# A fused windowed attention and feed-forward kernel: turning the probabilities by squares and through DRAM, with keys in classes of four

## The chip, the cores and the metric

The kernel runs on one core of a Trainium2 chip. A core has five engines that run side by side, each with its own instruction stream: TensorE (PE in the profile; PEld is its weight load) multiplies matrices out of SBUF into PSUM, VectorE (DVE), ScalarE (ACT) and GpSimd (POOL) work on tiles element by element, and SyncE (SP) issues the transfers between DRAM and SBUF. They wait for each other through semaphores. The metric is the device time of one execution in microseconds.

## The reference

What is computed, cut to what matters:

```
scores = q @ k^T / sqrt(64)                      # 8 batches x 8 heads, 576 tokens, head size 64
rel = pos_query - pos_key
heads 0-3: keep 0 <= rel < 32                    # a window
heads 4-7: keep 0 <= rel < 128 and rel % 4 == 0  # a window with dilation 4
attn = softmax(where(keep, scores, -1e9)) @ v
x = attn with the heads of a token side by side  # 4608 x 512
xn = x / sqrt(mean(x^2) + 1e-6) * rms_g
out = (silu(xn @ w_gate) * (xn @ w_val)) @ w_out # 512 -> 1536 -> 512
```

## The kernel before, in words

The 4608 tokens are cut into 16 units of 288 (half a batch). Attention and feed-forward are fused: while TensorE runs the feed-forward of one unit, the attention of the next is threaded between its matrix products.

The feed-forward of a unit runs over 12 blocks j of the hidden size. Each block has three parts, and each part is a **tick**: `gate` (12 large matmuls into the PSUM tile g), `val` (12 into v) and `proj` (12 into the four accumulators acc, for the block before). Large matmuls go in threes, since every fp32 operand is split into a high and a low part of a shorter type (L679 high by high, L682 the two mixed ones). So a unit has 36 ticks. Behind a gate ScalarE takes a tanh (L719) and VectorE makes of it a silu (L724); behind a val VectorE multiplies the two (L737, "the product"), ScalarE takes the high part (L748) and GpSimd the low part (L749). Two PSUM banks carry g and v in turns (`bank`): the gate of the next block is written where the val of this block lay, so it begins only when L737 has read it. The tile th has one buffer.

The attention of a unit is 14 **bursts** of two heads: for c = 0, 1 (window) three blocks of 96 queries each, with 128 keys (96 in the first block of an even unit); for c = 2, 3 (dilation) four residue classes of 72 queries, with 72 keys in even units and 104 in odd ones. Where a burst does its steps is written out by hand in ticks. `plan` puts the scores of burst k (s, L524) behind the large matmuls of tick −11 + 2k of its unit, the transposes (t, L497) 6 ticks later and the output (o, L512) 10 ticks later. So every second tick is heavy, with up to three such pieces on TensorE behind its 12 matmuls, and every other one light. What the other engines do is put off with `later(dt, rank, fn)`: `flush`, at the head of each tick, issues what is due in the order of rank. For a burst with its scores at tick n that is: n+1 the mask added to the low half of the scores (L381) and maximum (L386) on VectorE; n+2 two exponentials on ScalarE (L401); n+4 sum and reciprocal on VectorE (L410, L411) and scaling of the two heads on GpSimd (L417); n+6 two transposes on TensorE, through the matrix `ident`, into a PSUM tile (the free bank of g and v, or a tile t); a tick later `untranspose` copies it to SBUF as the high part (L477, ScalarE), and VectorE subtracts to make the low part (L479); n+10 the output, from high and low parts of probabilities (pt, two buffers) and of values (vhl, made by L320 on ScalarE and L324 on GpSimd); n+11 `take` adds the parts (L439, L441).

Queries and keys are loaded per head by SP (L293), and split by `split` into high and low: L349 and L354 for the keys (ScalarE, GpSimd), L358 and L363 for the queries. Values are loaded per burst (L301) into three buffers vt.

Units 0 to 2 run another way at the start (units with number below NEX = 3 keep exact probabilities, and their transposes). The 13 units from 3 on are the steady part. In them every engine's order is the order in which the program issues its instructions (a manual schedule).

## Time and profile before

| | us |
|---|---|
| median of three runs | 1104.16 (1103.92 to 1104.49) |
| the profiled execution's own time | 1103.95 |
| its span in the trace | 1102.2 |
| granted TensorE clock, mean | 1.0 of full speed |
| TensorE busy | 1095.2 |
| VectorE, ScalarE, GpSimd busy | 782.7, 614.8, 670.1 |
| bytes over the span | 73 GB/s |

The span runs from the first to the last record of the trace; the execution's own time is a little longer. A row of the grouped view names line, engine, operation, the tile written and the tiles read, shapes, count, then the sum of busy us and the mean ns of one, then the engine's idle time ahead of it. A row of the timeline gives start and duration in us; matmuls overlap in their pipeline, so for TensorE the distance from start to start tells what one costs.

### The profile page before, as it was taken

What the parts mean: (1) busy time and instruction counts of PE and PEld (TensorE: products, weight loads), DVE (VectorE), ACT (ScalarE), POOL (GpSimd) and SP (SyncE); (2) the same over time, 40 slices, a digit from 0 to 9 for tenths busy, and PEclk for the clock granted to TensorE, in tenths of its full rate; (3) what the DMA queues carried; (4) which work ended last, traced back from release to release, by engine and by line L of the source; (5) the groups of instructions that cost most, each with busy time, mean ns of one, the idle gap of its engine ahead of it and who ended that gap; (6) DMA issues with size and microseconds to landing.
All of it is one profiled execution on the core that took longest, in us unless ns stands there. A gap on an engine that the chain in (4) does not pass through costs nothing.

```text
span 1102.2 us, 25627 instructions
## 1 busy us (share of the span) xinstructions
PE 1095.2 (99%) x8416; PEld 1071.6 (97%) x8416; DVE 782.7 (71%) x3094; ACT 614.8 (56%) x2202; POOL 670.1 (61%) x1152
## 2 busy tenths in 40 slices
PE   8999999999999999999999999999999999999998
PEld 7787999999999999999999999999999999999998
DVE  7988667868687676867768677686867768687412
ACT  6895676556465564646556464664646556464211
POOL 6333589657585675757657575775758657584211
PEclk9999999999999999999999999999999999999999
DMA  9774213212131131312212131131212212120000
GB/s 255 205 263 163 79 51 87 74 35 82 43 94 52 41 97 30 95 42 73 66 36 85 43 94 43 50 96 37 79 43 83 64 32 83 53 74 13 18 6 22
DMA packets 61543, 82.18 MB, mean 75 GB/s; under 512 B 7298, under 2 KB 41090, under 8 KB 61410
## 3 DMA queue, kind: packets, MB, share of 16 engines
q1 hardware_dynamic: 61410, 80.54, 24.3%
q8 instruction: 67, 1.10, 0.4%
q14 instruction: 66, 0.54, 0.2%
HBM read 71.08 MB, written 9.44 MB: 73 GB/s over the span
## 4 chain that ended last, share of the span: by engine, by line
PE 95%; POOL 2%; DVE 1%; ACT 1%; issue 1%; POOLq 0%; ACTq 0%; DVEq 0%
PE acc L682 17%; PE g L682 17%; PE v L682 17%; PE acc L679 9%; PE g L679 9%; PE v L679 9%; PE o L512 3%; PE s L524 3%; PE acc L676 2%; PE v L676 2%; PE g L676 2%; PE t L497 2%; PE s L521 1%; PE g L497 1%; PE busy L802 1%; PE o L509 1%
## 5 line engine op out<-in xcount | busy, mean ns | idle before, releaser
L749 POOL TENSOR_TENSOR hlo<-th,hhi 128x288 fp32r<-128x288 f32 x179 | 145.2, 811 | 161.3 <-ACT hhi L748 147.8
L401 ACT ACTIVATE t<-t,sum 96x128 f32<-96x128 f32 (+3 forms) x448 | 165.9, 374 | 107.8 <-DVE sum L386 105.1
L682 PE MATMUL acc<-hhi,lo 128*128 128x288 f32 x720 | 212.7, 295 | 0.0
L417 POOL TENSOR_SCALAR t<-t,sum 96x128 f32<-96x128 f32 (+3 forms) x416 | 147.6, 366 | 88.4 <-DVE sum L411 74.6
L719 ACT ACTIVATE th<-g 128x288 f32<-128x288 f32 x180 | 73.8, 410 | 195.2 <-PE g L682 100.5
L682 PE MATMUL g<-xhi,lo 128*128 128x288 f32 x612 | 180.3, 295 | 0.0
L682 PE MATMUL v<-xhi,lo 128*128 128x288 f32 x612 | 180.2, 294 | 0.0
L439 DVE TENSOR_REDUCE xraw<-o 64x72 f32<-64x144 f32 (+1 forms) x364 | 117.1, 322 | 84.0 <-PE o L512 79.5
L724 DVE SCALAR_TENSOR_TENSOR th<-th,g 128x288 f32<-128x288 f32 x180 | 80.8, 449 | 102.0 <-ACT th L719 78.4
L682 PEld LDWEIGHTS acc<-hhi,lo 128*128 128x128 f32 x720 | 135.4, 188 | 0.0
L324 POOL TENSOR_TENSOR vhl<-vt,vhl 128x128 fp32r<-128x128 f32 x182 | 84.4, 464 | 70.4 <-ACT vhl L320 66.8
L748 ACT CAST hhi<-th 128x288 fp32r<-128x288 f32 x180 | 77.7, 432 | 75.5 <-DVE th L737 74.6
L682 PEld LDWEIGHTS g<-xhi,lo 128*128 128x128 f32 x612 | 115.2, 188 | 0.0
L682 PEld LDWEIGHTS v<-xhi,lo 128*128 128x128 f32 x612 | 115.1, 188 | 0.0
L737 DVE TENSOR_TENSOR th<-th,v 128x288 f32<-128x288 f32 x180 | 79.8, 444 | 43.6 <-PE v L682 43.5
L441 DVE TENSOR_TENSOR xraw<-o,xraw 64x72 f32<-64x72 f32 (+1 forms) x364 | 101.1, 278 | 12.5
L679 PE MATMUL acc<-hhi,hi_o 128*128 128x288 f32 x360 | 109.0, 303 | 0.0
L679 PE MATMUL g<-xhi,hi_g 128*128 128x288 f32 x357 | 107.0, 300 | 0.0
L682 PE MATMUL acc<-hlo,hi_o 128*128 128x288 f32 x360 | 106.4, 296 | 0.0
L363 POOL TENSOR_TENSOR qs<-qk,qs 64x288 fp32r<-64x288 f32 x104 | 84.3, 811 | 24.1 <-ACT qs L358 16.9
L354 POOL TENSOR_TENSOR ks<-qk,ks 128x288 fp32r<-128x288 f32 (+2 forms) x104 | 96.8, 936 | 3.1
L682 PE MATMUL g<-xlo,hi_g 128*128 128x288 f32 x322 | 95.1, 295 | 0.0
(193 smaller groups left out, 3458.6 us busy)
## 6 DMA issues: line engine op xcount, KB each, us to landing
qk<-in_qk_dram SPq DMA_DIRECT2D x60, 288.0 KB, 2.9
vt<-in_v_dram SPq DMA_DIRECT2D x196, 64.0 KB, 1.9
qk<-in_qk_dram SPq DMA_DIRECT2D x30, 352.0 KB, 2.9
out_dram<-ot SPq DMA_DIRECT2D x64, 144.0 KB, 1.9
qk<-in_qk_dram SPq DMA_DIRECT2D x30, 304.0 KB, 2.9
raw<-in_w_gate_dram SPq DMA_DIRECT2D x12, 512.0 KB, 4.6
...
```

The costliest lines, as they stand in the source:

```text
L324: G.tensor_tensor(out=vp[:, :, 1], in0=vs.pop(b), in1=vp[:, :, 0], op=ALU.subtract)
L354: ek.tensor_tensor(out=ks[:, 1, :nkt], in0=kr, in1=ks[:, 0, :nkt], op=ALU.subtract)
L363: eq.tensor_tensor(out=qs[D:], in0=qr[D:], in1=qs[D:], op=ALU.subtract)
L401: A.activation(out=t[:nq, a, :n], in_=t[:nq, a, :n], func=AF.Exp, scale=-1.0, bias=sm[:nq, a, 0:1], accum_out=None if by_rows(u, c, i) els ...
L417: (V if u == 0 and (c, i) > (NC - 1, 1) else G).tensor_scalar(out=t[:nq, a, :n], in0=t[:nq, a, :n], scalar1=sm[:nq, a, 3:4], scalar2=1.0, ...
L439: V.tensor_reduce(out=ours, in_=o[:D, cols:cols + 2 * nq].rearrange("d (t q) -> d q t", t=2), axis=mybir.AxisListType.X, op=ALU.add)
L441: V.tensor_tensor(out=ours, in0=o[D:, cols:cols + nq], in1=ours, op=ALU.add)
L679: PE.matmul(out, wh[:, cc, :], xh, start=start, stop=False)
L682: PE.matmul(out, w[:, cc, :], v, start=False, stop=stop and k == 1)
L724: V.scalar_tensor_tensor(out=t, in0=t, scalar=1.0, in1=g, op0=ALU.add, op1=ALU.mult)
L737: V.tensor_tensor(out=t, in0=t, in1=v_ps[:, :U], op=ALU.mult)
L749: (V if (u, j) == (NU - 1, NJ - 1) else G).tensor_tensor(out=lo, in0=t, in1=hi, op=ALU.subtract)
```

## The change

In units 3 to 15 the transposes on TensorE go. The scaled probabilities (a tile t of 96 queries by two heads by 128 keys) are turned in four steps instead. VectorE transposes t in place in squares of 32 x 32 (L514). SP writes it to a scratch tile in DRAM (L519). SP reads it back (L525) with the squares put in their places, in pieces of 32 floats: 128 partitions by 6 pieces. ScalarE makes the high part (L529), now from SBUF, and VectorE the low part (L533), now with both inputs in SBUF. The ticks are in `TURN`: squares and write at n+4, read-back at n+6, high part at n+8, low part at n+9, the output at n+10 as before. The scaling moves from n+4 to n+3.

In a square, 32 keys lie on 32 lanes, and the pieces that are read back hold, on each lane, the queries in a row. For this the 128 key places are seen as four classes of 32: the split of the keys (L351, L357) stores key 4i + c at place i of class c, the scores' matmul (L581) reads its keys by class, in runs of 18 to 32, and the mask is put into the same order once, ahead of unit 3. The tile t must hold no old numbers where a block has fewer than 96 queries or 128 keys: GpSimd zeroes it (L418) a tick ahead of the scores. vt goes from three buffers to two, and the loads of values and of queries and keys are issued a tick later.

The lines move: L737 is L799, L749 is L811, L719 L781, L724 L786, L679 and L682 are L741 and L744, L512 is L567, L524 L581, L439 and L441 L469 and L471, L381 L392, L386 L400, L401 L430, L410 and L411 L439 and L440, L417 L447, L293 L295, L301 L303.

```diff
-BEHIND = 6, 10
+OUTPUT = 10
+TURN = (4, 4), (4, 9.5), (6, 9.5), (8, 3), (9, -1.5)
...
+    dr = ctx.enter_context(tc.tile_pool(name="dr", bufs=2, space=bass.MemoryType.DRAM))
...
-            vt = sb.tile([P, 2, D], F32, tag="vt", name=f"vt_{u}_{c}_{i}", bufs=3)
+            vt = sb.tile([P, 2, D], F32, tag="vt", name=f"vt_{u}_{c}_{i}", bufs=2)
...
-            load_v(further(b, 3))
+            later(1, 9.9, lambda: load_v(further(b, 2)))
...
-            A.copy(out=ks[:, 0, :nkt], in_=kr)
+            A.copy(out=ks[:, 0, :nkt].rearrange("p (c k) -> p c k", c=4), in_=kr.rearrange("p (k c) -> p c k", c=4))
...
-            ek.tensor_tensor(out=ks[:, 1, :nkt], in0=kr, in1=ks[:, 0, :nkt], op=ALU.subtract)
+            hi, lo = (ks[:, t, :nkt].rearrange("p (c k) -> p c k", c=4) for t in range(2))
+            ek.tensor_tensor(out=lo, in0=kr.rearrange("p (k c) -> p c k", c=4), in1=hi, op=ALU.subtract)
...
-                load(*after(u, h, 2))
+                later(1, 9.9, lambda: load(*after(u, h, 2)))
...
+    def begin(b):
+        _, nq, _ = geometry(*b[:2])
+        n = geometry(*b[:2])[0][b[2]][3]
+        pool, bufs = (late[0], 1) if late and everything.index(b) % 4 == 3 else (sb, 3)
+        blank[b] = t = pool.tile([QB, 2, P], F32, tag="t", name=f"t_{b[0]}_{b[1]}_{b[2]}", bufs=bufs)
+        if nq < QB or n < P:
+            G.memset(t, 0.0)
...
-        def low_part():
-            V.tensor_tensor(out=pt[:n, 1, :, :nq], in0=t_in, in1=pt[:n, 0, :, :nq], op=ALU.subtract)
...
+    def turn(b):
+        blocks, nq, _ = geometry(*b[:2])
+        n = blocks[b[2]][3]
+        got = []
+
+        def squares():
+            t = st[b][0]
+            V.transpose(out=t, in_=t)
+
+        def put():
+            t, _ = st.pop(b)
+            d = dr.tile([2, QB, P], F32, tag="turn", name=f"turn_{b[0]}_{b[1]}_{b[2]}")
+            nc.sync.dma_start(out=d.rearrange("a q k -> q a k"), in_=t)
+            got.append(d)
+
+        def get():
+            st[b] = pt = sb.tile([P, 2, 2, QB], F32R, tag="pt", name=f"pt_{b[0]}_{b[1]}_{b[2]}", bufs=2)
+            squares = got.pop().rearrange("a (r i) (c j) -> (i c) (a r) j", i=W, j=W)
+            nc.sync.dma_start(out=pt[:, 1].bitcast(F32).rearrange("k a (r j) -> k (a r) j", j=W), in_=squares)
+
+        def high():
+            pt = st[b]
+            A.copy(out=pt[:n, 0, :, :nq], in_=pt[:n, 1, :, :nq].bitcast(F32))
+
+        def low():
+            pt = st[b]
+            V.tensor_tensor(out=pt[:n, 1, :, :nq], in0=pt[:n, 1, :, :nq].bitcast(F32), in1=pt[:n, 0, :, :nq],
+                            op=ALU.subtract)
+
+        for (dt, rank), fn in zip(TURN, (squares, put, get, high, low)):
+            later(dt, rank, fn)
...
-            PE.matmul(sv[:nq, a, :, :n], qs[:, qc:qc + nq], ks[:, :, kc:kc + n], start=True, stop=True)
+            nkt = geometry(*q[:2])[2]
+            kk = ks[:, :, :nkt].rearrange("p t (c k) -> p t c k", c=4)[..., kc // 4:(kc + n) // 4]
+            PE.matmul(sv[:nq, a, :, :n].rearrange("q t (c k) -> q t c k", c=4), qs[:, qc:qc + nq], kk,
+                      start=True, stop=True)
...
-            later(3 if q[0] < NNAT else 4, 1 if behind else -1, lambda: scores_norm(*q))
+            later(4 if q[0] == NNAT else 3, 1 if behind else 0.65 if q[0] >= NEX else -1, lambda: scores_norm(*q))
...
+                turn(q)
...
-        t_at, o_at = ([t + n for t in q_at] for n in BEHIND)
+        t_at, o_at = [None] * nb, [t + OUTPUT for t in q_at]
```

How the engines' orders move is seen in the attention of unit 8, which runs inside the feed-forward of unit 7. In the rows below stand the line, the operation, the tile written, the tiles read and the shape. The numbers behind t, pt, o, s, turn and vt are c and i of a burst; those behind th, g and v are the block j; that at the end counts buffers.

TensorE before, at the end of a heavy tick, from the last large matmuls of a proj to the first of the next gate:

```order
L682 MATMUL acc_3_8165<-hlo_2_8242,hi_g_1223 128x288
L682 MATMUL acc_3_8165<-hhi_2_8241,lo_1319 128x288
L512 MATMUL o_2_0_8361<-pt_2_0_8239,vhl_2294 128x144 x2
L497 MATMUL t_3_8359<-ident,t_2_2_8186 72x72 x2
L524 MATMUL s_3_1_8360<-ks_6_8037,qs_6_8076 72x2x72
L524 MATMUL s_3_1_8360<-ks_7_8074,qs_7_8116 72x2x72
L679 MATMUL g_4_8389<-xhi_0_7832,hi_g_1348 128x288
```

TensorE at the same place with the change:

```order
L744 MATMUL acc_3_8325<-hlo_2_8402,hi_g_1223 128x288
L744 MATMUL acc_3_8325<-hhi_2_8401,lo_1319 128x288
L567 MATMUL o_2_0_8529<-pt_2_0_8374,vhl_2301 128x144 x2
L581 MATMUL s_3_1_8528<-ks_6_8193,qs_6_8228 72x2x72
L581 MATMUL s_3_1_8528<-ks_7_8226,qs_7_8273 72x2x72
L741 MATMUL g_4_8552<-xhi_0_7980,hi_g_1348 128x288
```

The pair of transposes between o and s is gone; the rest keeps its order.

VectorE before, from the silu of block 3 to its product (L737), which the gate of block 4 waits for:

```order
L724 SCALAR_TENSOR_TENSOR th_3_8297<-th_3_8297,g_3_8276 128x288
L381 TENSOR_TENSOR t_3_0_8306<-s_3_0_8289,mask 72x2x72
L386 ISA t_3_0_8306,sum_88<-s_3_0_8289,t_3_0_8306 72x72
L386 ISA sum_88 72x1
L386 ISA t_3_0_8306,sum_88<-s_3_0_8289,t_3_0_8306 72x72
L386 ISA sum_88 72x1
L479 TENSOR_TENSOR pt_2_1_8299<-g_3_8276,pt_2_1_8299 72x2x72
L410 TENSOR_REDUCE sum_87<-sum_87 72x2
L411 RECIPROCAL sum_87<-sum_87 72x2
L737 TENSOR_TENSOR th_3_8297<-th_3_8297,v_3_8318 128x288
```

VectorE with the change, from the silu of block 3 (L786) past its product (L799):

```order
L786 SCALAR_TENSOR_TENSOR th_3_8462<-th_3_8462,g_3_8442 128x288
L439 TENSOR_REDUCE sum_89<-sum_89 72x2
L440 RECIPROCAL sum_89<-sum_89 72x2
L392 TENSOR_TENSOR t_3_0_8430<-s_3_0_8455,mask 72x8x18
L400 ISA t_3_0_8430,sum_90<-s_3_0_8455,t_3_0_8430 72x4x18
L400 ISA sum_90 72x1
L400 ISA t_3_0_8430,sum_90<-s_3_0_8455,t_3_0_8430 72x4x18
L400 ISA sum_90 72x1
L799 TENSOR_TENSOR th_3_8462<-th_3_8462,v_3_8482 128x288
L514 STREAM_TRANSPOSE t_2_3_8365<-t_2_3_8365 96x256
L533 TENSOR_TENSOR pt_2_1_8436<-pt_2_1_8436 72x2x72
```

In block 3 the low part has moved from ahead of the product to behind it, where the turn in squares stands too; sum and reciprocal have moved ahead of the mask. One block on, with the change, VectorE has:

```order
L786 SCALAR_TENSOR_TENSOR th_4_8567<-th_4_8567,g_4_8552 128x288
L514 STREAM_TRANSPOSE t_3_0_8430<-t_3_0_8430 96x256
L533 TENSOR_TENSOR pt_2_2_8510<-pt_2_2_8510 72x2x72
L799 TENSOR_TENSOR th_4_8567<-th_4_8567,v_4_8583 128x288
L469 TENSOR_REDUCE xraw_2_8535<-o_2_1_8597 64x72
```

There turn and low part stand ahead of the product, where before the product (L737) stood right behind the silu (L724).

SP's queue before, some four ticks of loads:

```order
L293 DMA qk_0_8114<-in_qk_dram 128x608
L301 DMA vt_2_1_8121<-in_v_dram 128x128
L293 DMA qk_1_8151<-in_qk_dram 128x608
L301 DMA vt_2_2_8192<-in_v_dram 128x128
L301 DMA vt_2_3_8255<-in_v_dram 128x128
```

SP's queue with the change, over about the same stretch:

```order
L525 DMA pt_1_2_8305<-turn_1_2_8234 128x6x32
L519 DMA turn_2_0_8307<-t_2_0_8142 96x2x128
L295 DMA qk_0_8309<-in_qk_dram 128x608
L303 DMA vt_2_0_8311<-in_v_dram 128x128
L295 DMA qk_1_8350<-in_qk_dram 128x608
L525 DMA pt_2_0_8374<-turn_2_0_8307 128x6x32
L519 DMA turn_2_1_8376<-t_2_1_8209 96x2x128
L303 DMA vt_2_1_8378<-in_v_dram 128x128
L525 DMA pt_2_1_8436<-turn_2_1_8376 128x6x32
```

Each burst now has a read-back (L525), behind it the write of the burst after (L519), and the loads behind these.

More of the change, by code (lines that the diff above doesn't have):

```diff
@@ L378, in scores_max @@
         other = u < NNAT and everything.index((u, c, i)) % 4 == 3
-        t = sb.tile([QB, 2, P], F32, tag="qs" if other else "t", name=f"t_{u}_{c}_{i}", bufs=3)
-        if u >= NEX:
-            V.tensor_tensor(out=t[:nq, :, :n], in0=sv[:nq, :, 1, :n],
-                            in1=mask[:nq, None, mc:mc + n].to_broadcast([nq, 2, n]), op=ALU.add)
+        if u < NEX:
+            t = sb.tile([QB, 2, P], F32, tag="qs" if other else "t", name=f"t_{u}_{c}_{i}", bufs=3)
+        else:
+            t = blank.pop((u, c, i))
+            tk, mk = keys(t, n), mask.rearrange("q (c k) -> q c k", c=4)[:, :, mc // 4:(mc + n) // 4]
+            low = sv[:, :, 1, :n]
+            if n == P:
+                mk = mk.rearrange("q c i -> q (c i)")[:, None]
+            else:
+                mk, low = mk[:, None], low.rearrange("q a (c i) -> q a c i", c=4)
+            V.tensor_tensor(out=tk[:nq], in0=low[:nq], in1=mk[:nq].to_broadcast(list(tk[:nq].shape)), op=ALU.add)
         sm = sums[everything.index((u, c, i)) % len(sums)]
         for a in range(2):
-            plus = t[:nq, a, :n] if u >= NEX else mask[:nq, mc:mc + n]
-            V.tensor_tensor_reduce(out=t[:nq, a, :n], in0=sv[:nq, a, 0, :n], in1=plus,
+            out, scores, plus = t[:nq, a, :n], sv[:nq, a, 0, :n], mask[:nq, mc:mc + n]
+            if u >= NEX:
+                out = plus = tk[:nq, a]
+                if n < P:
+                    scores = scores.rearrange("q (c i) -> q c i", c=4)
+            V.tensor_tensor_reduce(out=out, in0=scores, in1=plus,
                                    op0=ALU.add, op1=ALU.min,
@@ L390, in scores_max, with keys @@
         st[u, c, i] = t, sm
+    def keys(t, n):
+        return t[:, :, :n] if n == P else t.rearrange("q a (c i) -> q a c i", i=W)[..., :n // 4]
+    blank = {}
+    def begin(b):
[5 more added lines that the diff above has]
+            G.memset(t, 0.0)
     def by_rows(u, c, i):
@@ L400, in scores_exp @@
         for a in range(2):
-            A.activation(out=t[:nq, a, :n], in_=t[:nq, a, :n], func=AF.Exp, scale=-1.0,
+            e = t[:nq, a, :n] if u < NEX else keys(t, n)[:nq, a]
+            A.activation(out=e, in_=e, func=AF.Exp, scale=-1.0,
                          bias=sm[:nq, a, 0:1], accum_out=None if by_rows(u, c, i) else sm[:nq, a, 1:2])
@@ L416, in scores_norm @@
                 continue
+            e = t[:nq, a, :n] if u < NEX else keys(t, n)[:nq, a]
             (V if u == 0 and (c, i) > (NC - 1, 1) else G).tensor_scalar(
-                out=t[:nq, a, :n], in0=t[:nq, a, :n], scalar1=sm[:nq, a, 3:4],
+                out=e, in0=e, scalar1=sm[:nq, a, 3:4],
                 scalar2=1.0, op0=ALU.mult, op1=ALU.mult)
@@ L469, in attn_moe, with untranspose @@
     everything = [b for u in range(NU) for b in bursts(u)]
-    def untranspose(b, t_ps, wait):
+    def untranspose(b, t_ps):
         blocks, nq, _ = geometry(*b[:2])
         n = blocks[b[2]][3]
-        t_in = t_ps[:n].rearrange("k (a q) -> k a q", a=2)[:, :, :nq]
-        exact = b[0] < NEX
-        st[b] = pt = sb.tile([P, 2, 2, QB], F32 if exact else F32R, tag="pt", name=f"pt_{b[0]}_{b[1]}_{b[2]}", bufs=2)
-        A.copy(out=pt[:n, 0, :, :nq], in_=t_in)
-        def low_part():
-            V.tensor_tensor(out=pt[:n, 1, :, :nq], in0=t_in, in1=pt[:n, 0, :, :nq], op=ALU.subtract)
-        if not exact:
-            later(1, 0.4 if wait > 1 else -1.5, low_part) if wait else low_part()
+        st[b] = pt = sb.tile([P, 2, 2, QB], F32, tag="pt", name=f"pt_{b[0]}_{b[1]}_{b[2]}", bufs=2)
+        A.copy(out=pt[:n, 0, :, :nq], in_=t_ps[:n].rearrange("k (a q) -> k a q", a=2)[:, :, :nq])
+    def turn(b):
[23 more added lines that the diff above has]
+            later(dt, rank, fn)
     def products(q, t, o, t_ps, s_tag="s", o_tag="o", wait=0):
@@ L533, in products @@
         if t:
-            later(1, 0.2, lambda: untranspose(t, t_ps, wait))
+            later(1, 0.2, lambda: untranspose(t, t_ps))
         if o:
@@ L541, in products @@
             if o[0] < NEX:
-                later(1, 9, lambda: load_v(further(o, 3)))
+                later(1, 9, lambda: load_v(further(o, 2)))
             far = further(o, 2)
@@ L810, in plan @@
             for kind, t in zip("qto", ts):
-                events.setdefault(base + t, {})[kind] = b
+                if t is not None:
+                    events.setdefault(base + t, {})[kind] = b
         last = base + (o_at[-1] if u < NNAT else DONE)
@@ L816, in attend @@
     def attend(t_ps, **tags):
+        soon = events.get(now[0] + 1, {}).get("q", (0,))
+        if soon[0] >= NEX:
+            begin(soon)
         e = events.pop(now[0], {})
@@ L881, in attn_moe @@
                     free = None
-                if part == 2 or part == 1 and events.get(now[0], {}).get("t", (0,))[0] >= NEX:
-                    if "t" in events.get(now[0], {}):
-                        free = ps.tile([P, 512], F32, tag=bank("g", j), name=f"t_{u}_{j}")[:, :2 * QB]
+                if part == 2 and "t" in events.get(now[0], {}):
+                    free = ps.tile([P, 512], F32, tag=bank("g", j), name=f"t_{u}_{j}")[:, :2 * QB]
                 attend(free, s_tag="acc2" if t < 4 else "s", wait=(1, 2, 0)[part])
```

7 lines of the change are left out of this document (5 added, 2 removed).

## Prediction

> **What bounds the kernel now.** I read the page's busy times and its chain of work first.
>
> ```profile
> PE 1095.2 (99%) x8416; PEld 1071.6 (97%) x8416; DVE 782.7 (71%) x3094; ACT 614.8 (56%) x2202; POOL 670.1 (61%) x1152
> PE 95%; POOL 2%; DVE 1%; ACT 1%; issue 1%; POOLq 0%; ACTq 0%; DVEq 0%
> ```
>
> TensorE is busy for 99% of the span, and 95% of the chain that ended last is TensorE itself. Next I cut out one unit in the steady part, and inside it the stretch where the other engines are fullest. After the length come the busy us (and instructions) of PE, PEld, DVE, ACT and POOL, then the granted clock, the DMA share and GB/s.
>
> ```profile
> 501.00:566.70 65.70, 65.70 (x527) 65.69 (x526) 48.01 (x204) 36.64 (x137) 42.79 (x77) 1.00 0.21 62
> 512.50:532.00 19.50, 19.50 (x159) 19.50 (x158) 16.91 (x77) 12.27 (x49) 15.13 (x28) 1.00 0.34 107
> ```
>
> TensorE has no gap at a granted clock of 1.00, so a microsecond taken from its stream is a microsecond of time for as long as the others keep up. In the full stretch VectorE has 19.50 − 16.91 = 2.59 us to spare, GpSimd 4.37, ScalarE 7.23. How late may VectorE be? The product of gate and value (L737) frees the bank in which the next block's gate begins.
>
> ```profile
> 524.72 0.43 DVE L737 TENSOR_TENSOR th<-th,v 128x288 f32<-128x288 f32 x1
> ...
> 529.08 0.45 DVE L737 TENSOR_TENSOR th<-th,v 128x288 f32<-128x288 f32 x1 [0.43 <-PE v L682]
> ```
>
> ```profile
> 525.66 0.34 PE L679 MATMUL g<-xhi,hi_o 128*128 128x288 f32 x1
> ...
> 530.98 0.29 PE L679 MATMUL g<-xhi,hi_g 128*128 128x288 f32 x1
> ```
>
> The first product ends at 525.15, .51 us ahead of the gate; the second at 529.53, 1.45 ahead. Ticks go three to a block and two to a burst, so the picture repeats every two blocks: of a unit's 12 blocks I count 6 as tight.
>
> **Removed: the transposes on TensorE.** In 13 units of 14 bursts, 182 pairs (L497) go. I price a pair where TensorE's row of starts shows the same place with it and without.
>
> ```profile
> 502.98 0.29 PE L682 MATMUL acc<-hhi,lo 128*128 128x288 f32 x1
> 503.11 0.40 PE L524 MATMUL s<-ks,qs 128*96 128x256 f32 x2
> 503.35 0.29 PE L679 MATMUL g<-xhi,hi_o 128*128 128x288 f32 x1
> ...
> 510.21 0.30 PE L682 MATMUL g<-xhi,lo 128*128 128x288 f32 x1
> 510.34 0.33 PE L497 MATMUL g<-ident,t 96*128 96x96 f32 x2
> 510.45 0.45 PE L524 MATMUL s<-ks,qs 128*96 128x256 f32 x2
> 510.75 0.30 PE L679 MATMUL v<-xhi,hi_g 128*128 128x288 f32 x1
> ...
> 550.63 0.30 PE L682 MATMUL v<-xhi,lo 128*128 128x288 f32 x1
> 550.77 0.35 PE L512 MATMUL o<-pt,vhl 72*128 72x144 f32 x2
> 550.95 0.29 PE L497 MATMUL t<-ident,t 72*72 72x72 f32 x2
> 551.04 0.38 PE L679 MATMUL acc<-hhi,hi_o 128*128 128x288 f32 x1
> 551.26 0.29 PE L682 MATMUL acc<-hlo,hi_o 128*128 128x288 f32 x1
> ...
> 557.72 0.30 PE L682 MATMUL acc<-hhi,lo 128*128 128x288 f32 x1
> 557.85 0.34 PE L512 MATMUL o<-pt,vhl 72*128 72x144 f32 x2
> 558.03 0.34 PE L679 MATMUL g<-xhi,hi_g 128*128 128x288 f32 x1
> 558.21 0.30 PE L682 MATMUL g<-xlo,hi_g 128*128 128x288 f32 x1
> ```
>
> From the last large matmul to the next, s alone takes 503.35 − 502.98 = .37 and T with s .54: T is worth .17. With o, counted to the second large matmul, .63 against .49: .14. Its own place, start to start, is 510.45 − 510.34 = .11. I take .14, since o stands beside most pairs: 182 × .14 = 25.5 us, with ends 20.0 (.11) and 30.9 (.17). If everything else stays covered, the profiled execution's 1103.95 (its span of 1102.2 and 1.75 around it, which I leave alone; .2 below the runs' median) becomes **1078.5**.
>
> **Added on VectorE.** One turn of 96x256 in squares per burst. The trace has no such operation.
>
> ```profile
> L381 DVE TENSOR_TENSOR t<-s,mask 96x256 f32<-96x256 f32 x66 | 27.5, 417 | 1.2
> ...
> L479 DVE TENSOR_TENSOR pt<-t,pt 72x144 fp32r<-72x144 f32 x30 | 8.9, 296 | 0.6
> ```
>
> ```profile
> 514.78 0.26 DVE L441 TENSOR_TENSOR xraw<-o,xraw 64x96 f32<-64x96 f32 x1
> ```
>
> A pass over that very size takes .42 (L381). The lower end is .26, what VectorE takes for 96 elements a lane; the upper .83, two passes. I take .42. The full stretch holds 19.5/65.7 × 18 = 5.3 pairs of ticks, a burst each. There VectorE gains 5.3 × .42 = 2.2 of work while TensorE's time shrinks by 5.3 × .14 = .75: 19.1 us of work in 18.75. That is .4 over at the estimate, .45 under at .26, 2.5 over at .83.
>
> The low part (L479, now L533) subtracted with one input in PSUM; now both lie in SBUF, as in L660. What that does beside GpSimd can be read:
>
> ```profile
> 513.87 0.46 DVE L660 TENSOR_TENSOR xlo<-xraw,xhi 128x288 fp32r<-128x288 f32 x1 [0.17 <-ACT xhi L659]
> ...
> 179.97 0.70 DVE L660 TENSOR_TENSOR spare<-xraw,xhi 128x288 fp32r<-128x288 f32 x1
> ```
>
> ```profile
> 513.88 1.11 POOL L354 TENSOR_TENSOR ks<-qk,ks 128x288 fp32r<-128x288 f32 x1
> ...
> 521.38 0.80 POOL L354 TENSOR_TENSOR ks<-qk,ks 128x288 fp32r<-128x288 f32 x1
> ...
> 179.89 0.46 POOL L324 TENSOR_TENSOR vhl<-vt,vhl 128x128 fp32r<-128x128 f32 x1
> ```
>
> GpSimd's subtraction that starts .01 behind VectorE's takes 1.11 in place of .80; VectorE's that starts .08 behind GpSimd's takes .70 in place of .46. So a low part costs between 0 and .24 more on VectorE, and up to .31 on GpSimd. I take .12: 5.3 × .12 = .65 per unit. The Trainium skill has the rule (SBUF — State Buffer, "Who interferes with whom"): a VectorE instruction with two SBUF inputs and a GpSimd one that reads SBUF shut each other out for a whole instruction. The trace agrees in direction, with a smaller price than a whole instruction; the rule at its full word is the second rival.
>
> VectorE is thus over by .4 + .65 = 1.05 us in each unit's full stretch. What of it reaches TensorE is set by VectorE's order. In a tight block (th_3 in the rows of the change) the low part's .30 stood ahead of the product; low part and turn now stand behind it, so the product may come .51 + .30 = .8 late. In a loose block (th_4) both stand ahead of it, and its 1.45 shrinks to about .7. That leaves 1.05 − .8 = .25, to which I add .1 for gaps that VectorE cannot fill and .25 for GpSimd (next paragraph): .6 × 13 = 7.8. Forecast: 1078.5 + 7.8, or **1086**. Outside the stretch VectorE has (65.70 − 48.01) − 2.59 = 15.1 us free in 46.2, so it catches up before the next unit.
>
> **Added on GpSimd and ScalarE.** Eight bursts of a unit (72 queries), ten where a first block has only 96 keys, have their tile zeroed, and the low part of k reads with a stride.
>
> ```profile
> L263 POOL MEMSET qk<- x13: 572/599/681, 2.3 to 37.5; 64x576 f32 x5, 64x608 f32 x4, 64x704 f32 x4
> ```
>
> By elements 96x256 is .25, at most the .6 of these rows; ten are 2.5–6 us of 65.70 − 42.79 = 22.9 free. The eight strided subtractions of a unit, at 0 to half more than their .80, add 0–3.2. Most lies where GpSimd is free. But the turn waits for the scaling, which is asked for a tick sooner behind this work; where it comes late VectorE stands, 0–.5 us a unit: I take .25. The zeroing itself waits for the write of four bursts before, issued three ticks (5.5 us) earlier, landed by then. ScalarE's 29.06 free us hide its strided copies, and its copy of the high part was there before.
>
> **Moved, and the wait that is new.** SP now issues per burst a write and a read-back; the value and query-key loads stand a tick later behind them. The read-back waits for o of two bursts before, and behind it in the queue wait the next write and the loads. A value load, into two buffers now, has three ticks (3 × 65.7/36 = 5.5 us) to its use against 1.9 to land. ScalarE's copy of the high part waits for the landing, VectorE's low part for that, and o for both.
>
> ```profile
> vt<-in_v_dram SPq DMA_DIRECT2D x196, 64.0 KB, 1.9
> qk<-in_qk_dram SPq DMA_DIRECT2D x30, 304.0 KB, 2.9
> ```
>
> ```profile
> GB/s 0 0 0 0 0 0 0 0 0 0 5 108 174 210 144 16 0 0 0 0 0 0 0 0 0 0 0 0 0 0 0 0 0 0 0 0 0 0 0 0
> ```
>
> The second view is one value load in slices of .1 us: 128 packets of 512 B flow in about .45, the other 1.45 is fixed. The read-back moves 96 KB as 768 runs of 128 B. By bytes (1.0 us for 240 KB between the two rows) it lands in 1.9 + .13 ≈ 2.05; by packets at that load's rate in 1.45 + 6 × .45 = 4.15. I take 2.8. How much is free?
>
> ```profile
> 513.92 0.37 PE L512 MATMUL o<-pt,vhl 96*128 96x192 f32 x2
> ```
>
> ```profile
> 516.93 0.40 ACT L401 ACTIVATE t<-t,sum 96x128 f32<-96x128 f32 x1
> ...
> 517.62 0.18 ACT L401 ACTIVATION_READ_ACCUMULATOR t<-t,sum 96x1 f32 x1
> ```
>
> o ends at 514.29, and ScalarE reaches the copy's place behind these two exponentials at 517.80: 3.5 us. Anything that lands by then costs nothing. TensorE's s now takes its keys in runs of 18 to 32. Its starts above give .30 for a pair of 128x256, already in two runs; the price of more runs is 0, or at worst something like the .11 of a small matmul pair, 182 × .11 = 20 us. I take 0, the stream showing no charge for the second run.
>
> **The rivals.** *All covers hold*: the turn costs .26 to .35, or VectorE's lateness fits in the slack: 1078.5, within 1076 to 1080. For it: VectorE is busy 48.01 of 65.70 over a unit. Against: the sum in the full stretch.
>
> *The shared SBUF access is dearer*: each low part loses half a GpSimd subtraction of .80, that is .4, not .12. The excess becomes .4 + 5.3 × .4 = 2.5; less .8, plus the same .35, times 13: 26.7, or 1105. The broken runs of s at their worst (1086 + 20 = 1106) and a turn of two passes (2.5 + .65 − .8 + .35 = 2.7, 35 us: 1113) go with it: 1096 to 1113.
>
> *The read-back lands late, and the kernel is slower.* Beyond 3.5 us ScalarE stands, and VectorE's low part with it; beyond 3.5 + .75 (the room left to both kinds of block) = 4.25 every block pays, 12 × 13 = 156 us for each further one. That cancels the gain at 4.25 + 25.5/156 = 4.41; at 4.55 the time is 1078.5 + 47 = 1125. For it: the packet bound, 4.15, is near, and the write and loads of the same queue share the engines. Against: the bytes. A rule of the Trainium skill speaks for this rival (VectorE: DVE Perf Modes, "The three transpose paths"): a plain DMA that transposes by its access pattern is 19 times slower than the transposing one where the destination's innermost stride is large. Here the innermost 32 elements lie together on both sides, so its condition is not met; no row here shows such a transfer.
>
> **How the numbers follow.** Forecast (1080 to 1096) 50%, covers hold 18%, dearer SBUF and its companions 16%, late read-back 16%. The range: 1076 leaves out 4% below, 1107 the late read-back and little else, so 2 in 10. A measurement tells ±.2% (1102.0 to 1106.4) from no change. Faster: 50 + 18 + 7 of the third case = 75%; same 6%; slower 16 + 3 = 19%.
>
> **What would show it.** Right: no L497 rows in these units, a unit's period near 64.3, a turn of .42, the read-back's landing near 2.8, and TensorE's gaps only ahead of gates in the full stretch, released by the product on VectorE. Covers hold: no gaps at all. Late read-back: ScalarE's copy (L529) idle until a DMA lands. The forecast is wrong if TensorE's starts around s grow, or if the gaps are released by ScalarE or GpSimd.

## The result and the profile after

The changed kernel takes 1226.19 us (median of four runs, 1224.93 to 1227.04) against 1104.04 (1103.84 to 1104.49): the ratio is 1.1105, 95% interval 1.1086 to 1.1124. It is 122 us slower. The prediction had 1086 with a range of 1076 to 1107. The mean granted clock was .994 (1.0 before); on 1118.1 us of busy TensorE that is at most some 7 of the 122 us, by my estimate.

The page's busy times of the changed kernel, and two units of its steady part (columns as before):

```profile
PE 1118.1 (91%) x8052; PEld 1063.6 (87%) x8052; DVE 923.9 (75%) x3276; ACT 642.8 (52%) x2204; POOL 717.1 (59%) x1268
...
566.00:714.00 148.00, 133.02 (x985) 128.28 (x984) 117.79 (x434) 77.05 (x271) 93.86 (x171) 1.00 0.39 93
```

A unit takes 148.00 / 2 = 74.0 us, where it took 65.7 and the prediction had 64.3. TensorE, without a gap before, now stands 15 of 148 us. Yet no other engine is full: VectorE is busy 117.79 of 148.00, 80%, GpSimd 63%, ScalarE 52%. The time is lost to waits between engines that all have room. The view of waits names them (who, for whom, us in total, times, longest):

```profile
PE s L581 <- DVE sum L400: 56.5, 104, 1.1
DVE pt L533 <- ACT pt L529: 56.1, 107, 1.1
PE g L741 <- DVE th L799: 21.0, 26, 1.1
...
PE bps L690 <- DVE sum L439: 11.0, 13, 1.1
```

TensorE waits first of all at the scores (s, L581) for VectorE's maximum (L400) of the burst before: all scores share one PSUM bank, and it is free only when the maximum has read it. That is a wait the prediction did not name. The gate's wait for the product, which it did name, comes second. Third come 13 waits, one a unit, at bps, the matmul that spreads the norm's root (with the wait for ScalarE behind it, 17.9 us).

The groups of the new instructions, and the landings:

```profile
L514 DVE STREAM_TRANSPOSE t<-t 96x256 f32<-96x256 f32 x182 | 79.4, 436 | 17.6 <-POOL t L447 17.6
L533 DVE TENSOR_TENSOR pt<-pt 128x192 fp32r<-128x192 f32 x66 | 44.6, 676 | 16.0 <-ACT pt L529 16.0
L529 ACT CAST pt<-pt 72x144 fp32r<-72x144 f32 x48 | 14.6, 305 | 2.3 <-DMA pt<-turn 2.2
...
pt<-turn SPq DMA_DIRECT2D x182, 96.0 KB, 2.3
```

The turn takes .436 us (estimate .42). The read-back lands in 2.3 (estimate 2.8), and ScalarE's copy stood 2.2 us in all for it. The low part takes .67 in the mean of all shapes, twice what it took (.30 to .35 in L479).

How the waits hang together shows in one burst. VectorE, ScalarE, then TensorE:

```profile
652.30 0.37 DVE L392 TENSOR_TENSOR t<-s,mask 72x208 f32<-72x208 f32 x1
...
652.89 0.08 DVE L400 DVE_READ_ACCUMULATOR2_ANT sum<- 72x1 f32 x1
...
653.44 0.43 DVE L514 STREAM_TRANSPOSE t<-t 96x256 f32<-96x256 f32 x1
654.84 0.84 DVE L533 TENSOR_TENSOR pt<-pt 128x192 fp32r<-128x192 f32 x1 [0.96 <-ACT pt L529]
...
657.31 0.37 DVE L392 TENSOR_TENSOR t<-s,mask 72x208 f32<-72x208 f32 x1
```

```profile
653.05 0.38 ACT L430 ACTIVATE t<-t,sum 72x104 f32<-72x104 f32 x1 [1.47 <-POOL t L447]
...
654.13 0.42 ACT L810 CAST hhi<-th 128x288 fp32r<-128x288 f32 x1
654.46 0.35 ACT L529 CAST pt<-pt 128x192 fp32r<-128x192 f32 x1
```

```profile
653.30 0.40 PE L581 MATMUL s<-ks,qs 128*72 128x208 f32 x2 [1.01 <-DVE sum L400]
```

From mask to mask VectorE needs 657.31 − 652.30 = 5.0 us here. This is one of the longer bursts: over the two units a pair of ticks takes 148.00 / 36 = 4.1 us, where it took 65.7 / 18 = 3.65. VectorE is not full: behind the turn it stands .96 us at the low part, since ScalarE's high copy stands in its own queue behind two exponentials. Those wait for VectorE's maximum of a later burst. (Their row names GpSimd's scaling as the last releaser, but the first maximum is done at 652.89 + .08 = 652.97, .08 ahead of them.) So maximum, exponentials, high copy, low part, takes, reciprocal, next maximum form a ring through two in-order queues, and in this burst its length sets the time. VectorE waits at the low part in 107 of the 182 bursts (the view above); whether the ring is the bound there is what the runs test.

### The profile page after: what moved, and what is told of

Its sections match the earlier page's. It is cut to its first block, busy times and chain, and to the rows that moved or that the text cites. A ratio compares the mean times of both kernels' runs of the same rounds, so it can differ in the third digit from the quotient of the medians.

```text
span 1225.3 us, 26700 instructions
## 1 busy us (share of the span) xinstructions
PE 1118.1 (91%) x8052; PEld 1063.6 (87%) x8052; DVE 923.9 (75%) x3276; ACT 642.8 (52%) x2204; POOL 717.1 (59%) x1268
## 5 line engine op out<-in xcount | busy, mean ns | idle before, releaser
L430 ACT ACTIVATE t<-t,sum 96x128 f32<-96x128 f32 (+3 forms) x448 | 166.4, 375 | 215.5 <-POOL t L447 90.7
L811 POOL TENSOR_TENSOR hlo<-th,hhi 128x288 fp32r<-128x288 f32 x179 | 146.6, 819 | 201.3 <-ACT hhi L810 196.7
L447 POOL TENSOR_SCALAR t<-t,sum 96x128 f32<-96x128 f32 (+3 forms) x416 | 148.3, 369 | 193.3 <-DVE sum L440 158.5
L744 PE MATMUL acc<-hhi,lo 128*128 128x288 f32 x720 | 212.9, 296 | 0.0
L744 PE MATMUL v<-xhi,lo 128*128 128x288 f32 x612 | 181.4, 296 | 0.0
L744 PE MATMUL g<-xhi,lo 128*128 128x288 f32 x612 | 180.2, 294 | 0.0
L533 DVE TENSOR_TENSOR pt<-pt 128x192 fp32r<-128x192 f32 (+3 forms) x182 | 121.2, 666 | 56.4 <-ACT pt L529 56.1
L781 ACT ACTIVATE th<-g 128x288 f32<-128x288 f32 x180 | 73.4, 408 | 127.2 <-PE g L744 79.3
L786 DVE SCALAR_TENSOR_TENSOR th<-th,g 128x288 f32<-128x288 f32 x180 | 81.5, 453 | 75.3 <-ACT th L781 65.1
L744 PEld LDWEIGHTS acc<-hhi,lo 128*128 128x128 f32 x720 | 135.7, 188 | 0.0
L469 DVE TENSOR_REDUCE xraw<-o 64x72 f32<-64x144 f32 (+1 forms) x364 | 116.2, 319 | 9.6 <-PE o L567 7.1
L581 PE MATMUL s<-ks,qs 128*96 128x256 f32 (+3 forms) x364 | 69.8, 274 | 56.7 <-DVE sum L400 56.5
L741 PE MATMUL g<-xhi,hi_g 128*128 128x288 f32 x357 | 109.6, 307 | 7.5 <-DVE th L799 7.5
L744 PEld LDWEIGHTS v<-xhi,lo 128*128 128x128 f32 x612 | 116.3, 190 | 0.0
L744 PEld LDWEIGHTS g<-xhi,lo 128*128 128x128 f32 x612 | 115.2, 188 | 0.0
L357 POOL TENSOR_TENSOR ks<-qk,ks 128x288 fp32r<-128x288 f32 (+2 forms) x104 | 113.2, 1093 | 3.1
L471 DVE TENSOR_TENSOR xraw<-o,xraw 64x72 f32<-64x72 f32 (+1 forms) x364 | 101.0, 278 | 12.5
L741 PE MATMUL acc<-hhi,hi_o 128*128 128x288 f32 x360 | 108.9, 303 | 0.0
L744 PE MATMUL acc<-hlo,hi_o 128*128 128x288 f32 x360 | 106.7, 296 | 0.0
L581 PEld LDWEIGHTS s<-ks,qs 128*72 128x72 f32 (+1 forms) x364 | 43.8, 152 | 70.7 <-PE o L567 57.0
L799 DVE TENSOR_TENSOR th<-th,v 128x288 f32<-128x288 f32 x180 | 80.5, 447 | 23.3 <-PE v L744 20.5
```

The source lines that it names most:

```text
L357: ek.tensor_tensor(out=lo, in0=kr.rearrange("p (k c) -> p c k", c=4), in1=hi, op=ALU.subtract)
L430: A.activation(out=e, in_=e, func=AF.Exp, scale=-1.0, bias=sm[:nq, a, 0:1], accum_out=None if by_rows(u, c, i) else sm[:nq, a, 1:2])
L447: (V if u == 0 and (c, i) > (NC - 1, 1) else G).tensor_scalar(out=e, in0=e, scalar1=sm[:nq, a, 3:4], scalar2=1.0, op0=ALU.mult, op1=ALU.mult)
L469: V.tensor_reduce(out=ours, in_=o[:D, cols:cols + 2 * nq].rearrange("d (t q) -> d q t", t=2), axis=mybir.AxisListType.X, op=ALU.add)
L471: V.tensor_tensor(out=ours, in0=o[D:, cols:cols + nq], in1=ours, op=ALU.add)
L533: V.tensor_tensor(out=pt[:n, 1, :, :nq], in0=pt[:n, 1, :, :nq].bitcast(F32), in1=pt[:n, 0, :, :nq], op=ALU.subtract)
```

## The experiments

Each is the changed kernel with the edit shown; times are medians of two runs, with the ratio to the kernel before on the same chip. Three theories stood at first: LOOP (that ring), CAPACITY (VectorE has too much work) and ORDER (the reciprocal ahead of the maximum).

**The high copy first.**

```diff
-TURN = (4, 4), (4, 9.5), (6, 9.5), (8, 3), (9, -1.5)
+TURN = (4, 4), (4, 9.5), (6, 9.5), (8, 0.05), (9, -1.5)
```

> The high copy (L529) stands ahead of the two exponentials in its tick on ScalarE instead of behind them; nothing else moves. Theory LOOP: each burst, maximum on VectorE -> two exponentials on ScalarE -> high copy behind them -> low part on VectorE -> takes, silu, reciprocal, next maximum is a closed chain through two in-order queues, some 4.1 us long, and its length is the period of a burst. Then VectorE's idle time ahead of L533 (56 us) nearly goes and with up to .6 us x 182 less the time falls to 1120-1170. Theory CAPACITY: VectorE simply has too much work (low part .67 us instead of .35, turn .44); its work is unchanged, so the time stays within 1205-1230. Theory ORDER (the reciprocal ahead of the maximum): 1215-1230.

1210.07, ratio 1.0957 (1.0925 to 1.0988): 16 us, far less than LOOP had. Its waits say why.

```profile
ACT pt L529 <- DMA pt<-turn: 88.2, 73, 2.9
```

ScalarE now stands 88.2 us for the read-back and holds up the exponentials. The read-back itself is tied in, as it waits for the output of two bursts before, which frees its buffer. In the changed kernel SP's own waits show it:

```profile
SPq L525 <- PE o L567: 77.2, 75, 1.6
```

It needs the landing of its own write too (164.4 us in 114 waits of SP), but for the most part that comes before the output. I call that second ring READBACK.

**The low part on GpSimd.**

```diff
-            V.tensor_tensor(out=pt[:n, 1, :, :nq], ...
+            G.tensor_tensor(out=pt[:n, 1, :, :nq], ...
```

> The low part is subtracted by GpSimd instead of VectorE, in the same tick and rank. LOOP: VectorE waits for ScalarE's high copy no more, the chain is cut; 1105-1150. CAPACITY: VectorE's busy time falls by 182 x .67 = 121 us and the time by half of that or more: 1105-1165. ORDER: the time stays above 1190. All: GpSimd's busy time grows by 182 x .4 to .6, 73 to 110 us.

1176.24, ratio 1.065 (1.0607 to 1.0693): 50 us, outside every theory's range. The scores wait only 3.0 us, but the output waits for GpSimd's low part:

```profile
PEld o L567 <- POOL pt L533: 38.2, 44, 1.7
```

**The reciprocal behind the maximum.**

```diff
-... 0.65 if q[0] >= NEX else -1, lambda: scores_norm(*q))
+... 0.75 if q[0] >= NEX else -1, lambda: scores_norm(*q))
```

> Sum and reciprocal (L439, L440) stand behind the maximum of the next burst on VectorE instead of ahead of its mask (rank .75 instead of .65), so the scaling on GpSimd comes up to 1 us later. ORDER and LOOP: .33 us leave the chain ahead of the maximum, which the next scores wait for: up to 182 x .33 = 60 us less, 1165-1200. CAPACITY: the work is the same, 1215-1235.

1292.77, ratio 1.1705 (1.1671 to 1.1739): 67 us slower still, outside the range of all three theories. VectorE's turn now stands 82.7 us (17.6 with the change) for the scaling, which follows the reciprocal:

```profile
DVE t L514 <- POOL t L447: 82.7, 156, 0.9
```

So ORDER falls: the sooner reciprocal helps this path. By how much stays open, for two other things moved too. The mean granted clock is .967 (.994 with the change), and TensorE is busy for 1158.9 us with the same matmuls (1118.1); and the low parts take 159.8 us in all at their old place (121.2).

**No turn in squares.**

```diff
-        for (dt, rank), fn in zip(TURN, (squares, put, get, high, low)):
+        for (dt, rank), fn in list(zip(TURN, (squares, put, get, high, low)))[1:]:
```

> The turn in squares on VectorE is left out (write, read-back, high and low part stay), so the output is not the reference's. CAPACITY: 182 x .436 = 79 us of VectorE's work go, the time falls by 60-80: 1145-1165. LOOP: half of the turns run while VectorE would wait for the high copy; the time falls by less than 45: 1180-1225. ORDER: over 1190.

1210.66, ratio 1.0962 (1.0918 to 1.1006). 79.4 us of VectorE's work went, the time fell by 15.5, in LOOP's range. CAPACITY falls. The gap is taken up by waiting for ScalarE, and the scores wait as before:

```profile
DVE pt L533 <- ACT pt L529: 112.3, 144, 1.5
...
PE s L581 <- DVE sum L400: 55.4, 103, 1.1
```

**All of the change but the turn.** TensorE transposes as before, from tiles in the order of the classes; the value rows are loaded in that order.

```diff
-                turn(q)
...
-        t_at, o_at = [None] * nb, [t + OUTPUT for t in q_at]
+        t_at, o_at = [t + 6 for t in q_at], [t + OUTPUT for t in q_at]
...
+                nc.sync.dma_start(out=out, in_=rows.rearrange("(k c) x -> c k x", c=4))
```

> All parts of the change except the turn: keys in classes of four, zeros, scaling a tick sooner, two value buffers, later loads; the probabilities are turned by TensorE's transposes as before (the rows of the values are loaded in the order of the classes). Theory TURN (the path through VectorE's squares, DRAM and back costs all of the loss): 1098-1112, as before the change. Theory PARTS (the slower splits of keys on ScalarE and GpSimd, L351 .70 to .96 us where it was .43, or the scores' broken runs, cost much): over 1120.

1144.13, ratio 1.0361 (1.0331 to 1.0391): 40 us of loss without the turn. TensorE, then GpSimd, around the norm of a unit:

```profile
523.03 0.30 PE L726 MATMUL g<-xhi,lo 128*128 128x288 f32 x1
524.03 0.37 PE L672 MATMUL bps<-rd,ones 96*128 96x288 f32 x1 [0.70 <-DVE sum L445]
524.93 0.40 PE L672 MATMUL bps<-rd,ones 96*128 96x288 f32 x1 [0.53 <-ACT rd L656]
525.17 0.30 PE L723 MATMUL v<-xhi,hi_o 128*128 128x288 f32 x1
```

```profile
519.74 0.67 POOL L453 TENSOR_SCALAR t<-t,sum 96x96 f32<-96x96 f32 x2 [2.49 <-DVE sum L446]
520.50 0.81 POOL L372 TENSOR_TENSOR qs<-qk,qs 64x288 fp32r<-64x288 f32 x1
521.38 0.94 POOL L363 TENSOR_TENSOR ks<-qk,ks 128x288 fp32r<-128x288 f32 x1
522.28 0.87 POOL L638 TENSOR_TENSOR rst<-rst,mhalf 96x3 f32<-96x3 f32 x1
```

GpSimd stands 2.49 us at the scaling for VectorE's reciprocal, then does the splits that it used to do in that time, and only then the power for the norm (L638). From the gate's last matmul to the val's first, 525.17 − 523.03 = 2.14 us pass. The kernel before, at the same place:

```profile
504.80 0.29 PE L682 MATMUL g<-xhi,lo 128*128 128x288 f32 x1
504.93 0.43 PE L628 MATMUL bps<-rd,ones 96*128 96x288 f32 x2
505.20 0.29 PE L679 MATMUL v<-xhi,hi_o 128*128 128x288 f32 x1
```

That is .40, so 1.74 us a unit or 23 in 13. I call this HEAD: an instruction issued sooner than its input is ready stands at the head of its queue.

**The low part at the end of its tick**, then that with the high copy first, then the low part on GpSimd with the high copy first.

```diff
-(8, 3), (9, -1.5)
+(8, 3), (9, 0.8)       # low_behind
+(8, 0.05), (9, 0.8)    # low_behind_hi
+(8, 0.05), (9, -1.5)   # hi_lowg, low part on GpSimd
```

> The low part (L533) stands at the end of its tick on VectorE, behind the maximum, instead of at its head; all else as with the change. LOOP (maximum -> exponentials -> high copy -> low part -> takes -> maximum is a closed chain through VectorE's and ScalarE's queues): the low part leaves the chain, VectorE's idle time ahead of L533 (56 us) goes and the maximum comes earlier by the low part's .67 and that wait: 60 to 110 us less, 1115-1165. READBACK (what counts is output of two bursts before -> read-back -> high -> low -> output, since the probabilities have two buffers): the low part comes some 1.5 us later, the output waits for it: 1215-1280.

1189.24, ratio 1.077 (1.0735 to 1.0804). 37 us, between the theories.

```profile
PE o L567 <- DVE pt L533: 34.7, 38, 2.3
```

The wait of the scores for the maximum is gone (.2 us), and the output waits for the low part in its stead. The move did a second thing: at its new place the low part meets GpSimd less often, and its rows take 84.9 us in all (121.2 with the change). So the 37 us are not the order's alone.

> Both: the low part behind the maximum and the high copy ahead of the exponentials. LOOP: no slower than the low part behind alone, 1105-1165. READBACK: ScalarE stands for the landing (88 us in the run with the high copy first) and its exponentials come late: 1190-1260.

1207.33, ratio 1.0933 (1.0902 to 1.0965): in READBACK's range.

> The low part on GpSimd and the high copy ahead of the exponentials. With the low part on GpSimd alone (1176) TensorE's output waited 66 us for it. LOOP: the high copy comes up to .8 us sooner, most of those 66 us go: 1120-1155. READBACK: the landing sets when the high copy runs, so little changes: 1165-1185.

1184.7, ratio 1.0728 (1.0697 to 1.076), no better than the low part on GpSimd alone. READBACK's range again: the high copy cannot come sooner than the landing lets it, and ScalarE stands 127.6 us for it.

**The scaling at other places.** First in the kernel with TensorE's transposes (all of the scaling back at n+4), then in the changed kernel (at n+4 with turn and write at n+5), alone and with the low part on GpSimd or at the end of its tick.

```diff
-            later(4 if q[0] == NNAT else 3, 1 if behind else 0.65 if q[0] >= NEX else -1, lambda: scores_norm(*q))
+            later(3 if q[0] < NNAT else 4, 1 if behind else -1, lambda: scores_norm(*q))   # pe_turn_norm4
...
+                later(1, -1, lambda a=a, e=e: G.tensor_scalar(out=e, in0=e, ...))   # scale_late and its two
...
-TURN = (4, 4), (4, 9.5), ...
+TURN = (5, 0.9), (5, 9.5), ...   # scale_late and its two
```

> TensorE's transposes kept as in pe_turn (1144), and sum, reciprocal and scaling put back to n+4, rank -1. Theory HEAD (in pe_turn the scaling, asked for a tick sooner, stands at the head of GpSimd's queue and waits for VectorE's reciprocal, while key and query splits and the power for the norm queue up behind it; TensorE's gap ahead of bps, 23 us in 13 units, is its price): 1102-1112, no gap ahead of bps. Theory PARTS (strided splits, zeros): 1120 or more.

1116.61, ratio 1.0113 (1.0084 to 1.0142). The sooner scaling was worth 1144.1 − 1116.6 = 27.5 us, and of the 17.9 us of waits at bps .5 are left: HEAD holds in that form, though its range ended at 1112. Some 12 us stay.

> As with the change, but GpSimd's scaling is issued at the head of tick n+4 (sum and reciprocal stay at n+3), and squares and write follow at n+5. HEAD: the gap ahead of bps (23 us) goes: 1185-1205, while the maximum is as late as before. LOOP alone: 1215-1235. READBACK: the write lands later, the read-back with it: over 1235.

1223.13, ratio 1.1078 (1.1046 to 1.111): the wait at bps goes and the time hardly moves, as LOOP alone had it.

> The same with the low part on GpSimd (that alone: 1176, with 23 us ahead of bps and 34 us in which the output waits for GpSimd's low part). HEAD and LOOP: both go in good part: 1110-1145. READBACK: 1160-1200.

1146.15, ratio 1.0381 (1.0299 to 1.0462), just above HEAD and LOOP's range. This is the fastest form with the turn that I found, and still 42 us behind the kernel before; ScalarE's high copy (L533 in this form) stands for the landing:

```profile
ACT pt L533 <- DMA pt<-turn: 111.1, 102, 3.0
SPq L529 <- DMA turn<-t: 251.4, 164, 3.6
```

Here it is not READBACK: the write leaves a tick later, and the read-back (L529 in this form) waits for its landing; for an output it waits once, 1.5 us. This form's two runs lie 7.5 us apart.

> The same with the low part on VectorE, behind the maximum (that alone: 1189, with 23 us ahead of bps and 65 us in which the output waits for the low part). HEAD and LOOP: 1140-1170. READBACK (two probability buffers leave four ticks from read-back to output, the low part comes too late in them): 1165-1200.

1181.37, ratio 1.07 (1.0661 to 1.0738), READBACK's range, though here too the read-back waits for the write's landing.

**The scaling at the end of its tick**, behind the splits, with turn and write where the change has them; then with the low part on GpSimd, later in its tick; then with the high copy sooner as well.

```diff
+                later(3, 5.5, lambda: scale(*q))
                 turn(q)
...
-(8, 3), (9, -1.5)
+(8, 3), (9, 1)      # scale_mid_lowg
+(8, 0.55), (9, 1)   # scale_mid_lowg_hi
```

> As with the change, but GpSimd's scaling stands at the end of tick n+3 (behind the splits of keys, queries and values) instead of at its head; squares and write stay at n+4. HEAD: the 23 us ahead of bps go, nothing else is delayed: 1190-1210. LOOP says that the maximum stays late (o to s some 65 us). If the squares wait for the later scaling as in norm_behind (1293), over 1230.

1219.1, ratio 1.1043 (1.1011 to 1.1075). HEAD had 1190 to 1210: in the full path the wait at bps falls from 17.9 to 6.0 us and that at the scores from 56.5 to 49.0, the output's rises from 3.1 to 10.6, and 7 us of time are all that comes of it.

> The same with the low part on GpSimd, behind hlo in its tick. Against scale_late_lowg (1146) the write leaves a tick sooner. READBACK: the sooner write lets the read-back land sooner, ScalarE's 111 us of standing for it go in part: 1110-1140. If GpSimd's length of queue governs: 1140-1160.

1183.39, ratio 1.0719 (1.0688 to 1.075), outside both ranges and 37 us behind scale_late_lowg. The turn stands 105.5 us on VectorE for the later scaling, and the output 44.7 us for GpSimd's low part (9.6 in scale_late_lowg, where that stands at the head of its tick):

```profile
DVE t L523 <- POOL t L458: 105.5, 129, 3.0
```

> The same with the high copy right behind ScalarE's copy of the feed-forward, ahead of the splits: the low part gets its input up to 1 us sooner, if the landing allows it. READBACK (landing governs): no faster than scale_mid_lowg, within 10 us. LOOP: 10 to 30 us less.

1184.37, ratio 1.0728 (1.0697 to 1.0759): no difference.

**The low part with one SBUF input**, to take the contention with GpSimd away: a multiplication by 0, then a reduction over one element (which passes the values through).

```diff
-            V.tensor_tensor(out=pt[:n, 1, :, :nq], in0=..., in1=pt[:n, 0, :, :nq], op=ALU.subtract)
+            V.tensor_scalar(out=pt[:n, 1, :, :nq], in0=..., scalar1=0.0, scalar2=1.0, ...)   # low_one_input
+                V.tensor_reduce(out=pt[:n, 1, :, :nq], in_=...[:, :, :, None], ...)          # low_reduce
```

> As with the change, but the low part on VectorE is a multiplication by 0 with one SBUF input in place of the subtraction with two; same place, same waits. The low parts of the probabilities are left out of the output. CONTENTION (the low part takes .67 us instead of .31 because it waits for GpSimd at the shared SBUF access, and it stands in the chain of the maximum): L533 falls to .35 or less, the time by up to 182 x .35 = 64 us: 1155-1185, and o to s gaps shrink from 65 us to under 30. If only the waiting for ScalarE's high copy counts: over 1205.

1212.38, ratio 1.0963 (1.0926 to 1.0999). It did not do what it was for: the group takes .60 us, against .67.

> As with the change, but in place of the subtraction VectorE passes the values through a reduction over one element (one SBUF input): same place, same waits; the low part of the probabilities is replaced by the values themselves, so the output is not the reference's. low_one_input left L533 at .60 us (.23 alone, .72 beside GpSimd), took 14.6 us off VectorE's work and 13.8 us off the time, so it did not take the contention away. CONTENTION: if this form runs at .25 to .35 whatever GpSimd does, 182 x .35 = 64 us leave the chain: 1150-1180, o to s gaps under 30 us. If VectorE then only stands longer for ScalarE's high copy: 1195-1215.

1180.5, ratio 1.0688 (1.065 to 1.0727), half a microsecond outside CONTENTION's range.

```profile
L534 DVE TENSOR_REDUCE pt<-pt 128x192 fp32r<-128x192 f32 x66 | 21.8, 330 | 14.8 <-ACT pt L529 14.3
...
PE s L582 <- DVE sum L400: 35.2, 92, 1.0
```

VectorE's work fell from 923.9 to 858.5 us, by 65, and the time by 46: of a microsecond of low part .7 reach the time, of a microsecond of turn .2 (15.5 of 79.4). The low part lies in the ring, the turn for the most part in its waits.

**No zeros**, in the form with TensorE's transposes and the scaling at n+4.

```diff
-        if nq < QB or n < P:
-            G.memset(t, 0.0)
```

> pe_turn_norm4 (1116.6; transposes on TensorE, scaling back at n+4) without GpSimd's zeroing, which that form does not need. If the zeros (116 x .31 us on GpSimd) cause the 12 us that were left to the kernel before: 1104-1109. If the strided splits of the keys do (ScalarE .72 us instead of .43, GpSimd .96 instead of .84): 1112-1118.

1114.76, ratio 1.008 (1.0051 to 1.0109) against 1.0113 (1.0084 to 1.0142) with zeros. The intervals overlap; most of the 12 us does not come from the zeros. The strided split of the keys is the likelier source. It was not tried alone, and neither was the load of the value rows in the order of the classes, which only the forms with TensorE's transposes have:

```profile
L351 ACT CAST ks<-qk 128x288 fp32r<-128x288 f32 x48 | 33.5, 711 | 0.0
...
L357 POOL TENSOR_TENSOR ks<-qk,ks 128x288 fp32r<-128x288 f32 x48 | 46.9, 981 | 1.4
```

Before, these took 429 ns (L349) and 843 (L354).

## Why the prediction was wrong

**What bounds the kernel.** Right: TensorE's stream without gaps, so that every wait of TensorE is time.

**The transposes.** Right. At 638.51 in the changed kernel, a place with o and s and no wait:

```profile
638.51 0.30 PE L744 MATMUL acc<-hhi,lo 128*128 128x288 f32 x1
638.64 0.36 PE L567 MATMUL o<-pt,vhl 128*128 128x192 f32 x2
638.84 0.40 PE L581 MATMUL s<-ks,qs 128*96 128x256 f32 x2
639.08 0.37 PE L741 MATMUL g<-xhi,hi_g 128*128 128x288 f32 x1
```

.57 us pass, where o and s with T took 514.53 − 513.79 = .74 in the kernel before:

```profile
513.79 0.30 PE L682 MATMUL acc<-hhi,lo 128*128 128x288 f32 x1
...
514.53 0.30 PE L679 MATMUL g<-xhi,hi_g 128*128 128x288 f32 x1
```

That is .17, within the prediction's .11 to .17.

**VectorE's sum: the step that failed.** The prediction added up VectorE's work in the full stretch, set it against the time there (1.05 us over), took off what the product may be late (.8) and let .25 reach TensorE: with .35 for gaps and GpSimd, 7.8 us in all. Measured, the time is 148 us above its 1078.5. Three things were wrong with it.

First, it let VectorE's lateness reach TensorE through the product alone. The scores' bank, freed by the maximum, was left out, and there the largest wait is: 56.5 us in 104 waits.

Second, it counted work and free time, as if an engine with 20% to spare could be no later than its work makes it. But the low part was put at the head of a light tick on VectorE, behind a high copy that stands behind two exponentials on ScalarE. The runs show this: taking away 79.4 us of turn gave 15.5, while moving the low part to the end of its tick gave 37, and the scores' wait went. Part of the 37 is the shorter low part there; but low_reduce, with a low part as short at the old place, still had 35.2 us of the scores' wait, so that wait goes with the place.

Third, the low part's .12 for contention was mis-sized; it measured some .34 (a mean of .67, against .31 alone in the two smaller shapes and .36 in 128x192), outside the bound of .24. In the prediction's own sum .34 gives 1101, so this alone does not explain 1226: most of the miss is the path. The bound came from one row in which GpSimd's instruction had only .38 us to go. Four places in the changed kernel, VectorE then GpSimd:

```profile
214.73 0.31 DVE L533 TENSOR_TENSOR pt<-pt 104x144 fp32r<-104x144 f32 x1 [0.62 <-ACT pt L529]
...
219.11 0.81 DVE L533 TENSOR_TENSOR pt<-pt 104x144 fp32r<-104x144 f32 x1 [0.59 <-ACT pt L529]
...
596.33 0.31 DVE L533 TENSOR_TENSOR pt<-pt 72x144 fp32r<-72x144 f32 x1 [0.18 <-ACT pt L529]
...
611.22 0.31 DVE L533 TENSOR_TENSOR pt<-pt 72x144 fp32r<-72x144 f32 x1
```

```profile
218.94 0.81 POOL L811 TENSOR_TENSOR hlo<-th,hhi 128x288 fp32r<-128x288 f32 x1 [0.42 <-ACT hhi L810]
...
595.66 0.81 POOL L366 TENSOR_TENSOR qs<-qk,qs 64x288 fp32r<-64x288 f32 x1
...
610.55 0.80 POOL L811 TENSOR_TENSOR hlo<-th,hhi 128x288 fp32r<-128x288 f32 x1 [1.07 <-ACT hhi L810]
```

Alone (214.73) it takes .31; begun .17 behind a hlo of .81 it takes .81, what is left of hlo and some .17 more. Begun with only .14 or so of GpSimd's instruction to go (596.33 and 611.22) it takes .31 again. The prediction's row fits: .24 more with .38 to go. The Trainium skill's rule (SBUF — State Buffer, "Who interferes with whom"), that such a pair shut each other out for a whole instruction, was the right one here; the prediction had taken the one smaller row for the price, and left the rule at its full word to its second rival. By low_reduce the contention is worth 46 of the 122 us.

**The scaling a tick sooner.** It was put at 0 to 6.5 us, as work on GpSimd that comes late. It cost 27.5 in pe_turn, and not as work: GpSimd stood 2.49 us for the reciprocal with splits and the norm's power queued behind it. The prediction looked at what waits for the scaling, not at what is queued behind it.

**The read-back.** The landing was well sized (2.3 for 2.8), and the rival that the 128-byte pieces land late was wrong: ScalarE's copy stood 2.2 us for it. The Trainium skill's warning against transposing by access pattern (VectorE: DVE Perf Modes, "The three transpose paths") did not bear, as the prediction said. The late read-back, the rival with the right sign, thus had the wrong mechanism, and the dearer SBUF access had a right mechanism with a price that left out the ring (1105). The read-back counts another way: with two buffers for the probabilities it leaves after the output of two bursts before. The forms that asked for the high copy ahead of the exponentials met that path next (ScalarE stood 88.2 us for the landing in high_first, 127.6 in hi_lowg). In the forms with the later write it was the write's landing that held the read-back (111.1 in scale_late_lowg). Where the high copy kept its place, ScalarE's wait stayed short (17.7 us in low_gpsimd, 18.3 in low_behind), and the output waited for the low part.

**Keys in classes.** Put at nothing; with the other parts that stay in pe_turn_norm4 they cost some 12 us, most of it not the zeros. Which of these parts costs it stays open.

**What stays open.** The prices do not add up, since what one cure frees returns at the next wait: scale_mid took 11.9 us off the waits at bps and gained 7. How much a third buffer for the probabilities would give was not tried and HEAD was not taken away alone in the full path without moving other waits. No form with the turn came near the kernel before; the best lost 42 us.
